# First-chunk keys without copies, bounds buffers cleared on VectorE, and some gelu casts on ScalarE, in a fused attention and MLP kernel

## The chip, the cores and the metric

The kernel runs on one core of a Trainium2 chip. The metric is the device time of one execution in microseconds, median over runs. The engines are TensorE (PE, with its weight loads as PEld), VectorE (DVE), ScalarE (ACT), GpSimd (POOL) and SyncE (SP); transfers are issued from SP's and ScalarE's queues.

## What is computed

Attention over 4 batches, 8 heads, 768 positions and 64 elements a head, in which a query sees the first `n_global` keys and a window of `n_local` keys behind it, with a slope by distance for each head; then a two-layer MLP with exact gelu over the 3072 rows of 512.

```python
scores = scale * np.matmul(q, k.transpose(0, 1, 3, 2))
keep = is_global | is_local                     # key < n_global, or 0 <= q - k < n_local
scores = np.where(keep, scores + bias, -1e9)    # bias = -slope_h * distance
a = softmax(scores);  x = np.matmul(a, v)       # then (B*S, H*D) = (3072, 512)
h = x @ w_in                                    # 512 -> 2048
g = 0.5 * h * (1.0 + erf(h / sqrt(2)))
out = g @ w_out                                 # 2048 -> 512
```

The weights come as 64-bit words; the kernel decodes them itself.

## The kernel before

The rows are cut into 12 chunks `c` of 256 queries, three to a batch. The attention of a chunk goes by four pairs of heads `p`. `scores_pair` multiplies queries and keys in two halves `j` of 128 queries, for each head `hh` and each half `a` of 64 queries. The keys of such a half are 192 columns: 64 near, 32 global and 96 near. In the chunks that begin a batch they are picked out of a row of keys with copies behind it (`kr`, with `KW + 96` columns). One reduction on VectorE (L373) adds the masks `pens` and takes the row maxima into `nmax`. `exps` takes exponentials on ScalarE (L402) with sums `su`; then come the sum's inverse (L404, L405) and the scaling of `n` (L411), on VectorE in chunks 0 and 1 and on GpSimd after that. `flip` transposes on TensorE (L423) and copies to `pt` on ScalarE (L427), `av_pair` multiplies with the values (L461) and splits the result into a high and a low part of `x` in fp16 (L503 or L510 on ScalarE, L191 on VectorE).

The MLP goes by slices `s` of 256 of the 2048 columns, eight of them, in steps `T`: first the slices of chunks 0 and 1 in turn, then the other chunks. `m1` is the first layer (L537, and L531 for chunks 0 and 1 from slice 2 on), `gelu` takes the gelu on ScalarE into `gr` (L553) and splits it into `gh` (L554) and `gl` (L192) on VectorE, `m2` is the second layer (L581, L566). Each slice's weights come in four pieces; `split_weights` and `part_weights` decode a piece with one instruction on ScalarE (L227), three on VectorE (L233, L235, L237), a cast on ScalarE (L247) and a rest on VectorE (L192), into `winh`, `winl`, `wouth`, `woutl`. Slice 0 is decoded beside the attention of chunks 0 and 1, the others up to about step 14. `warm` issues products whose result nobody reads, as many as the table `FILL` says, between those of the first attention.

`consts` builds the masks: row and column numbers by GpSimd, casts on VectorE (L150, L151), the two limits by a transfer (L80, used from L86 on), and eight scaled masks `pens` (L168). The buffers `xtop`, `xlow`, `wtop` and `wlow` hold running bounds from step 15 on; they are cleared in `consts` by GpSimd.

Each engine serves its own list in order. The lists are not the order of the code: a scheduler lays the instructions out by its own estimate of their times, with some orders given by hand (`after`, `behind`, `table`). A small change of the code can so change the lists elsewhere.

## Time and profile before

| | us |
|---|---|
| median of 3 runs | 648.76 (648.11 to 650.12) |
| the profiled execution, its own time | 647.65 |
| its span, first to last instruction | 645.8 |
| TensorE busy | 628.7 (97%) |
| VectorE busy | 369.2 (57%) |
| ScalarE busy | 313.0 (48%) |
| GpSimd busy | 80.4 (12%) |

Times in the trace are counted from the span's start. A busy share is a mean over stages: VectorE is busy without a break from about 50 to 120 us and half idle after that. The chain of work that ended last says which engine was waited for.

### The profile page before, as it was taken

The numbers are of one execution on the slowest core, as the hardware profiler recorded it, in microseconds if no ns is written. First come the engines' busy times: TensorE is split into PE (matmuls) and PEld (weight loads), VectorE is DVE, ScalarE is ACT, GpSimd is POOL, SyncE is SP. The second block draws the span as 40 slices with busy tenths as digits, with TensorE's granted clock in tenths as the row PEclk, the third lists the DMA queues.
The fourth block names the chain that finished last, engine by engine and source line by source line (L and its number), as shares of the span: only waits on it lengthen the run. The fifth ranks groups of instructions, "written<-read, shape, count | busy, mean of one in ns | idle before, by whom it ended". The sixth has DMA issues, their size and how long they took to land.

```text
span 645.8 us, 14522 instructions
## 1 busy us (share of the span) xinstructions
PE 628.7 (97%) x5712; PEld 424.3 (66%) x5712; DVE 369.2 (57%) x1160; ACT 313.0 (48%) x757; POOL 80.4 (12%) x175
## 2 busy tenths in 40 slices
PE   8998999999999999999999999999999999999995
PEld 5555544457777676676776767677776767767663
DVE  8989999955546546436436436435435445342622
ACT  3786586735535526526526436355355355362210
POOL 3000005301202102101002022021011021020000
PEclk9998999999999999999999999999999999999998
DMA  8949825314504415304235145034064062000001
GB/s 256 261 177 266 262 73 192 115 37 144 171 24 143 119 56 162 113 37 147 80 94 165 49 124 165 11 138 133 17 172 128 37 172 66 33 2 1 34 1 38
DMA packets 66187, 71.27 MB, mean 110 GB/s; under 512 B 32704, under 2 KB 49344, under 8 KB 66112
## 3 DMA queue, kind: packets, MB, share of 16 engines
q1 hardware_dynamic: 61664, 62.93, 32.2%
q10 hardware_dynamic: 4448, 7.34, 3.2%
q8 instruction: 47, 0.77, 0.5%
q14 instruction: 28, 0.23, 0.1%
HBM read 63.97 MB, written 6.29 MB: 109 GB/s over the span
## 4 chain that ended last, share of the span: by engine, by line
PE 84%; DVE 9%; ACT 4%; issue 1%; DMA 1%; POOL 0%; POOLq 0%; ACTq 0%; DVEq 0%
PE h L537 33%; PE acc L581 32%; PE av L461 5%; PE t L423 5%; PE s L362 4%; PE h L531 2%; PE acc L566 2%; DVE wb L235 2%; ACT n L402 1%; DVE wb L237 1%; DVE wb L233 1%; DVE n L373 1%; DVE gl L192 1%; DVE ta L150 1%; DVE winl L192 1%
## 5 line engine op out<-in xcount | busy, mean ns | idle before, releaser
L537 PE MATMUL h<-x,winh 128*128 128x256 f16 x1344 | 228.3, 274 | 0.9 <-ACT x L503 0.4
L537 PE MATMUL h<-x,winl 128*128 128x256 f16 x672 | 184.0, 274 | 0.0
L554 DVE TENSOR_SCALAR gh<-gr 128x512 f16<-128x512 f32 x96 | 42.7, 445 | 213.6 <-ACT gr L553 213.6
L537 PEld LDWEIGHTS <-winh 128*128 128x128 f16 x1344 | 131.5, 98 | 32.9 <-issue 1.4
L411 POOL TENSOR_SCALAR n<-n,su 128x192 f32<-128x192 f32 (+1 forms) x160 | 75.2, 489 | 494.3 <-ACT n L402 240.2
L553 ACT ACTIVATE gr<-h 128x512 f32<-128x512 f32 x96 | 57.3, 597 | 153.9 <-issue 87.3
L581 PE MATMUL acc<-wouth,gl 128*128 128x512 f16 x336 | 127.0, 379 | 1.0 <-DVE gl L192 1.0
L581 PE MATMUL acc<-wouth,gh 128*128 128x512 f16 x336 | 127.5, 380 | 0.1
L581 PE MATMUL acc<-woutl,gh 128*128 128x512 f16 x336 | 127.3, 379 | 0.0
L581 PEld LDWEIGHTS <-gh 128*128 128x128 f16 x672 | 64.2, 98 | 66.0 <-issue 4.3
L427 ACT COPY pt<-t 128x384 f32<-128x384 f32 x96 | 45.1, 475 | 93.7 <-PE t L423 92.0
L537 PEld LDWEIGHTS <-winl 128*128 128x128 f16 x672 | 66.1, 98 | 9.7 <-issue 0.8
L192 DVE SCALAR_TENSOR_TENSOR gl<-gr,gh 128x512 f16<-128x512 f32 x96 | 66.7, 694 | 8.5
L402 ACT ACTIVATE n<-n,mn 128x192 f32<-128x192 f32 (+1 forms) x144 | 62.1, 432 | 4.1 <-DVE mn L373 3.9
L581 PEld LDWEIGHTS <-gl 128*128 128x128 f16 x336 | 32.9, 98 | 41.0 <-DVE gl L192 1.5
L373 DVE CUSTOM_DVE_ANT_0 n<-s,pens 128x192 f32<-128x192 f32 (+1 forms) x192 | 54.9, 341 | 0.1
L423 PE MATMUL t<-ident,n 128*128 128x128 f32 x288 | 47.8, 276 | 3.2 <-DVE n L411 2.4
L461 PE MATMUL av<-pt,vr 64*64 64x64 f32 (+2 forms) x1312 | 42.4, 250 | 2.0 <-ACT pt L427 2.0
L461 PEld LDWEIGHTS av<-pt,vr 64*64 64x64 f32 (+1 forms) x1312 | 35.4, 134 | 11.5 <-issue 8.0
L423 PEld LDWEIGHTS t<-ident,n 128*128 128x128 f32 x288 | 34.7, 142 | 8.5 <-DVE n L411 2.4
L362 PE MATMUL s<-kr,qr 64*64 64x192 f32 (+2 forms) x752 | 39.1, 323 | 0.7 <-DMA kr<-kT 0.7
L261 DVE SCALAR_TENSOR_TENSOR wand<-c,wand 128x128 int32<-128x128 int32 x128 | 37.5, 293 | 2.7
(108 smaller groups left out, 595.9 us busy)
## 6 DMA issues: line engine op xcount, KB each, us to landing
w<-w SPq DMA_DIRECT2D x32, 512.0 KB, 6.3
c<-w SPq DMA_DIRECT2D x32, 512.0 KB, 5.6
out<-o ACTq DMA_DIRECT2D x23, 256.0 KB, 2.0
qr<-qT SPq DMA_DIRECT2D x11, 512.0 KB, 4.2
vr<-v SPq DMA_DIRECT2D x22, 256.0 KB, 4.4
kr<-kT SPq DMA_DIRECT2D x16, 320.0 KB, 4.9
vr<-v SPq DMA_DIRECT2D x19, 192.0 KB, 2.9
kr<-kT SPq DMA_DIRECT2D x36, 64.0 KB, 3.3
```

Of the source, the lines that this page charges most:

```text
L192: return self.nc.vector.scalar_tensor_tensor(out=out, in0=in_, scalar=scale, in1=hi, op0=ALU.mult, op1=ALU.subtract)
L362: ins = nc.tensor.matmul(out, lhsT=lhs, rhs=rhs, start=True, stop=True).ins
L373: ins = nc.vector.tensor_tensor_reduce(out=nn[:, j * NK:j * NK + n], in0=sp[hh][:, j, 0:n], in1=self.pens[:, 2 * p + hh, o:o + n], scale=- ...
L402: self.table(nc.scalar.activation(out=nn, in_=nn, func=AF.Exp, bias=mn[:, i:i + 1], scale=-1.0, accum_out=su[:, i:i + 1]))
L411: ins = eng.tensor_scalar(out=nn, in0=nn, scalar1=su[:, i:i + 1], scalar2=0.0, op0=ALU.mult, op1=ALU.add)
L423: self.last_t = nc.tensor.transpose(tp[:, i, :], nn[:, o:o + P], self.ident).ins
L427: ins = nc.scalar.copy(pt, tp).ins
L461: ins = nc.tensor.matmul(out, lhsT=lhs, rhs=rhs, start=start, stop=stop, skip_group_check=True).ins
L537: ins = nc.tensor.matmul(hp[:, f, :], lhsT=w[:, d, fs], rhs=x[:, d, e, :], start=n == 0, stop=n == 3 * NP - 1).ins
L553: self.table(nc.scalar.activation(out=gr, in_=hp, func=AF.Gelu, scale=1.0 / (WS * XS)))
L554: nc.vector.tensor_scalar(out=gh, in0=gr, scalar1=GS, scalar2=None, op0=ALU.mult)
L581: ins = nc.tensor.matmul(acc, lhsT=g[:, f, ks], rhs=w[:, f, :], start=s == 0 and n == 0, stop=(s == NST - 1 or (c, s) == (NCH - 1, NST - 2 ...
```

## The change

Three edits, and the order of instructions that follows from them.

Chunk 0 keeps only its 256 columns of keys, without copies behind them, so two transfers (96 and 32 columns of all four pairs) are not issued. In its second half (`c == 0`, `j == 1`) each product of 192 columns becomes three, of 64, 32 and 96 columns, with the same weights and neighbouring results. `FILL` loses its entry between the two halves of pair 0, and gives 5 and 7 products instead of 4 and 9 behind pairs 0 and 1. The four bounds buffers are cleared on VectorE at step 14 instead of on GpSimd in front. And from slice 2 on the cast to `gh` is done by ScalarE for chunks 0 and 1, which is twelve steps.

```diff
-FILL = {(0, 0, 0): 4, (0, 0, 1): 4, (0, 1, 1): 9, (0, 2, 1): 4, (0, 3, 1): 4, (1, 0, 1): 4}
+FILL = {(0, 0, 1): 5, (0, 1, 1): 7, (0, 2, 1): 4, (0, 3, 1): 4, (1, 0, 1): 4}
...
-        for m in (self.xtop, self.xlow, self.wtop, self.wlow):
-            nc.gpsimd.memset(m, 0.0)
...
-        kr = self.es.tile([P, NP, KW + 96], F32, name="kr0")
+        kr = self.es.tile([P, NP, CT], F32, name="kr0")
...
-        nc.sync.dma_start(kr[:, 0, 0:CT], dap(self.kT, 0, [[S, P], [1, CT]]))
+        nc.sync.dma_start(kr[:, 0], dap(self.kT, 0, [[S, P], [1, CT]]))
         nc.scalar.dma_start(qr[:, 1:NP], dap(self.qT, P * S, [[S, P], [P * S, NP - 1], [1, CT]]))
-        nc.sync.dma_start(kr[:, :, CT:CT + 96], dap(self.kT, 0, every + [[1, 96]]))
-        nc.sync.dma_start(kr[:, :, CT + 96:], dap(self.kT, 0, every + [[1, NG]]))
-        nc.sync.dma_start(kr[:, 1:NP, 0:CT], dap(self.kT, P * S, [[S, P], [P * S, NP - 1], [1, CT]]))
+        nc.sync.dma_start(kr[:, 1:NP], dap(self.kT, P * S, [[S, P], [P * S, NP - 1], [1, CT]]))
...
+                    elif c == 0:
+                        x = 2 * P - HQ if a else NG
+                        parts = [(out[:, 0:NX], kt[hr, x:x + NX]), (out[:, NX:NX + NG], kt[hr, 0:NG]),
+                                 (out[:, NX + NG:], kt[hr, NC:2 * NC])]
...
+                    for out, rhs in parts:
+                        ins = nc.tensor.matmul(out, lhsT=lhs, rhs=rhs, start=True, stop=True).ins
...
-        nc.vector.tensor_scalar(out=gh, in0=gr, scalar1=GS, scalar2=None, op0=ALU.mult)
+        if STEPS[t][0] < CAT and STEPS[t][1] > 1:
+            nc.scalar.activation(out=gh, in_=gr, func=AF.Copy, scale=GS)
+        else:
+            nc.vector.tensor_scalar(out=gh, in0=gr, scalar1=GS, scalar2=None, op0=ALU.mult)
...
+            if T == 14:
+                for m in (self.xtop, self.xlow, self.wtop, self.wlow):
+                    self.behind(self.nc.vector.memset(m, 0.0))
```

The lists change in many places. First VectorE's, at the first two pairs of heads (`n_0` to `n_3` are the scores of heads 0 to 3 of chunk 0, `su` their sums). Before:

```order
L404 TENSOR_SCALAR su_0_262<-su_0_262 128x4
L373 ISA n_2_313,nmax<-s_2_296,pens 128x128
...
L405 RECIPROCAL su_0_262<-su_0_262 128x4
L373 ISA n_3_316,nmax<-s_3_297,pens 128x192
...
L411 TENSOR_SCALAR n_0_279<-n_0_279,su_0_262 128x128
```

Now:

```order
L404 TENSOR_SCALAR su_0_256<-su_0_256 128x4
L405 RECIPROCAL su_0_256<-su_0_256 128x4
L411 TENSOR_SCALAR n_0_278<-n_0_278,su_0_256 128x128
...
L373 ISA n_2_318,nmax<-s_2_295,pens 128x128
```

The scaling of heads 0 and 1 has moved ahead of the reductions of heads 2 and 3.

Then VectorE's, where the second chunk begins (`n_0`, `n_1` and `su_0` are now those of chunk 1, `n_7` is chunk 0's last head, `wb_1` to `wb_3` are pieces of the first slice). Before, the reductions of chunk 1's heads 0 and 1 stand ahead of all this:

```order
L411 TENSOR_SCALAR n_7_435<-n_7_435,su_3_419 128x192
L192 SCALAR_TENSOR_TENSOR winl_330<-wb_1_393,winh_329 128x512
L233 TENSOR_SCALAR wb_2_451<-w_2_186 128x512
L404 TENSOR_SCALAR su_0_477<-su_0_477 128x4
L191 TENSOR_TENSOR x<-av_2_466,x 128x256
L235 SCALAR_TENSOR_TENSOR wb_2_451<-w_2_186,wb_2_451 128x512
L405 RECIPROCAL su_0_477<-su_0_477 128x4
L237 ISA wb_2_451<-w_2_186,wb_2_451 128x1024
L411 TENSOR_SCALAR n_0_492<-n_0_492,su_0_477 128x192 x2
```

Now:

```order
L411 TENSOR_SCALAR n_7_456<-n_7_456,su_3_432 128x192
L190 SCALAR_TENSOR_TENSOR winl_335<-wb_1_406,winh_334 128x512
L231 TENSOR_SCALAR wb_2_472<-w_2_180 128x512
L233 SCALAR_TENSOR_TENSOR wb_2_472<-w_2_180,wb_2_472 128x512
L235 ISA wb_2_472<-w_2_180,wb_2_472 128x1024
L373 ISA n_0_513,nmax<-s_0_499,pens 128x192
...
L404 TENSOR_SCALAR su_0_498<-su_0_498 128x4
L405 RECIPROCAL su_0_498<-su_0_498 128x4
L411 TENSOR_SCALAR n_0_513<-n_0_513,su_0_498 128x192 x2
```

The four reductions of chunk 1's first pair now stand behind the decoding of piece 2, directly ahead of the sum that waits for their exponentials. (Lines behind the diff's first edits are numbered a few lower or higher in the new kernel.)

Last, ScalarE's list at a step with exponentials between the gelu and its cast (`n_0`, `n_1` are scores of chunk 2). Before:

```order
L553 ACTIVATE gr_1187<-h_1172 128x512
L402 ACT_TABLE_LOAD
L402 ACTIVATE n_0_1140,su_0_1129<-n_0_1140,nmax 128x192 x2
L402 ACTIVATE n_1_1143,su_0_1129<-n_1_1143,nmax 128x192 x2
L247 ACTIVATE wouth_993<-wb_3_1057 128x512
L247 ACTIVATE winh_1096<-wb_0_1101 128x512
```

Now:

```order
L553 ACTIVATE gr_1208<-h_1193 128x512
L402 ACT_TABLE_LOAD
L402 ACTIVATE n_0_1161,su_0_1150<-n_0_1161,nmax 128x192 x2
L402 ACTIVATE n_1_1164,su_0_1150<-n_1_1164,nmax 128x192 x2
L245 ACTIVATE winh_1117<-wb_0_1122 128x512
L225 ACTIVATE w_2_238<-w_2_238 128x512
L225 ACTIVATE w_3_240<-w_3_240 128x512
L555 ACTIVATE gh_1206<-gr_1208 128x512
```

The cast to `gh` stands behind the exponentials and three weight instructions.

## Rows read from the trace of the kernel before

**Rows 1.** The page's chain of work that ended last, by engine

```profile
PE 84%; DVE 9%; ACT 4%; issue 1%; DMA 1%; POOL 0%; POOLq 0%; ACTq 0%; DVEq 0%
```

**Rows 2.** Timeline of VectorE, 0 to 16 us: start, us, engine, line, operation

```profile
1.77 4.04 DVE L150 CAST ta<-tb 128x320 f32<-128x320 int32 x1 [0.22 <-POOL tb L147]
...
6.19 0.16 DVE L86 CAST nn_f<-nn_w 128x4 f32<-128x4 int32 x1
...
10.48 0.29 DVE L373 CUSTOM_DVE_ANT_0 n<-s,pens 128x128 f32<-128x128 f32 x1
```

**Rows 3.** Timeline of GpSimd: the last of the four clears

```profile
4.67 0.96 POOL L170 MEMSET wlow<- 128x1024 f16 x1
```

**Rows 4.** Timeline of ScalarE's queue, and transfers to 40 us with median time to landing

```profile
0.74 0.42 ACTq L80 DMA_DIRECT2D nn_w<-limits  x1
...
nn_w<-limits ACTq DMA_DIRECT2D x1, 2.0 KB, 3.7
```

**Rows 5.** The chain in order of time, 0 to 67 us: start, us, what

```profile
10.81 1.76 ACT n L402 x8
...
14.81 0.56 ACT w L227
15.36 0.37 ACT pt L427
...
16.21 0.91 PE s L362 x12
...
18.67 0.96 PE av L461 x14
...
28.89 0.38 DVE x L191
...
29.96 0.64 DVE wb L237
...
31.52 0.34 DVE wb L233
...
32.45 0.60 DVE wb L235
```

**Rows 6.** Timeline of VectorE: the scaling of four pairs ends where these begin

```profile
20.18 0.17 DVE L404 TENSOR_SCALAR su<-su 128x4 f32<-128x4 f32 x1 [1.32 <-ACT n L402]
...
21.45 0.69 DVE L192 SCALAR_TENSOR_TENSOR winl<-wb,winh 128x512 f16<-128x512 f32 x1
...
31.43 0.42 DVE L233 TENSOR_SCALAR wb<-w 128x512 int32<-128x512 int32 x1
...
36.60 0.42 DVE L233 TENSOR_SCALAR wb<-w 128x512 int32<-128x512 int32 x1
```

**Rows 7.** Timeline of TensorE, 66 to 140 us: its gaps, with who ended them

```profile
100.95 0.44 PE L423 MATMUL t<-ident,n 128*128 128x128 f32 x2 [0.76 <-POOL n L411]
...
122.28 0.59 PE L531 MATMUL h<-x,winh 128*128 128x512 f16 x2 [0.42 <-DVE x L191]
```

**Rows 8.** Groups by line: the page's, and those of 5 to 60 us by shape

```profile
L554 DVE TENSOR_SCALAR gh<-gr 128x512 f16<-128x512 f32 x96 | 42.7, 445 | 213.6 <-ACT gr L553 213.6
...
L247 ACT ACTIVATE winh<-wb 128x512 f16<-128x512 f32 x5 | 3.1, 624 | 0.1
```

**Rows 9.** TensorE's timeline at 29.78, and busy time by window with PEclk, granted clock

```profile
29.78 0.43 PE L461 MATMUL av<-pt,vr 128*64 128x128 f32 x2 [1.42 <-ACT pt L427]
...
31.00:32.00 1.00, 1.00 (x11) 0.43 (x4) 1.00 (x5) 0.26 (x1) 0.00 (x0) 0.50 0.93 340
```

**Rows 10.** TensorE's timeline: six transposes; and their weight loads, 5 to 60 us

```profile
14.19 1.00 PE L423 MATMUL t<-ident,n 128*128 128x128 f32 x6 [0.26 <-DVE n L411]
...
L423 PEld LDWEIGHTS t<-ident,n 128*128 128x128 f32 x48 | 5.7, 144 | 5.0 <-DVE n L411 2.4 <-ACT pt L427 0.7 <-issue 0.7
```

**Rows 11.** The chain in order of time, 67 to 160 us

```profile
111.18 2.71 PE h L531 x12
...
114.59 1.28 ACT L402
```

More of the change, by code (lines that the diff above doesn't have):

```diff
@@ L267, in load_first @@
         nc = self.nc
-        kr = self.es.tile([P, NP, KW + 96], F32, name="kr0")
+        kr = self.es.tile([P, NP, CT], F32, name="kr0")
         qr = self.es.tile([P, NP, CT], F32, name="qr0")
         vr = self.es.tile([P, 4, DM], F32, name="vr0")
-        every = [[S, P], [P * S, NP]]
         nc.sync.dma_start(qr[:, 0], dap(self.qT, 0, [[S, P], [1, CT]]))
-        nc.sync.dma_start(kr[:, 0, 0:CT], dap(self.kT, 0, [[S, P], [1, CT]]))
+        nc.sync.dma_start(kr[:, 0], dap(self.kT, 0, [[S, P], [1, CT]]))
         nc.scalar.dma_start(qr[:, 1:NP], dap(self.qT, P * S, [[S, P], [P * S, NP - 1], [1, CT]]))
-        nc.sync.dma_start(kr[:, :, CT:CT + 96], dap(self.kT, 0, every + [[1, 96]]))
-        nc.sync.dma_start(kr[:, :, CT + 96:], dap(self.kT, 0, every + [[1, NG]]))
-        nc.sync.dma_start(kr[:, 1:NP, 0:CT], dap(self.kT, P * S, [[S, P], [P * S, NP - 1], [1, CT]]))
+        nc.sync.dma_start(kr[:, 1:NP], dap(self.kT, P * S, [[S, P], [P * S, NP - 1], [1, CT]]))
         self.vr[0] = vr
@@ L351, in scores_pair @@
                     if c == 0 and j == 0:
-                        out, lhs, rhs = sp[hh][:, 0, 0:P], qq[hr, 0:P], kt[hr, 0:P]
-                    elif first and j == 0:
-                        out, rhs = out[:, 0:P], kt[hr, 0:P]
-                    else:
-                        if first:
-                            rhs = pairs(kt[hr, :], 192 if a else 288, -96 if a else -192, NC)
-                        elif j == 0:
-                            rhs = pairs(kt[hr, :], 96, 96 if a else -96, NC)
-                        else:
-                            rhs = pairs(kt[hr, :], KW + 192 * a, -96 if a else 96, NC)
-                    ins = nc.tensor.matmul(out, lhsT=lhs, rhs=rhs, start=True, stop=True).ins
-                    if prev is not None:
-                        self.after(ins, prev, "heads and halves in turn")
-                    prev = ins
+                        parts = [(sp[hh][:, 0, 0:P], kt[hr, 0:P])]
+                        lhs = qq[hr, 0:P]
+                    elif c == 0:
+                        x = 2 * P - HQ if a else NG
+                        parts = [(out[:, 0:NX], kt[hr, x:x + NX]), (out[:, NX:NX + NG], kt[hr, 0:NG]),
+                                 (out[:, NX + NG:], kt[hr, NC:2 * NC])]
+                    elif first and j == 0:
+                        parts = [(out[:, 0:P], kt[hr, 0:P])]
+                    elif first:
+                        parts = [(out, pairs(kt[hr, :], 192 if a else 288, -96 if a else -192, NC))]
+                    elif j == 0:
+                        parts = [(out, pairs(kt[hr, :], 96, 96 if a else -96, NC))]
+                    else:
+                        parts = [(out, pairs(kt[hr, :], KW + 192 * a, -96 if a else 96, NC))]
+                    for out, rhs in parts:
+                        ins = nc.tensor.matmul(out, lhsT=lhs, rhs=rhs, start=True, stop=True).ins
+                        if prev is not None:
+                            self.after(ins, prev, "heads and halves in turn")
+                        prev = ins
             if (c, p, j) in FILL:
```

## The prediction

> **What bounds the kernel now.** I read the chain of work that ended last first: 84% of the span is TensorE [rows 1]. From about 62 us on its products follow one another almost without a gap; later work that is made shorter on another engine is worth only the gaps it closes. Then I read the chain's first 67 us and the timelines of the first 60: there TensorE waits for a ring in which VectorE reduces the scores of a pair of heads (L373), ScalarE takes the exponentials (L402), VectorE scales them (L404 to L411), TensorE transposes and multiplies, and VectorE decodes weight words (L233, L235, L237) in between. So the time is the length of the head, plus TensorE's gaps behind it, plus fixed TensorE work. The change touches the first two.
>
> **No clearing on GpSimd.** VectorE's cast of the row numbers (L150) takes 4.04 us for 320 columns [rows 2], while GpSimd clears four buffers, the last until 5.63 [rows 3]. Without them the cast should fall well under 1 us. Not all of that is gained: the third instruction behind it, L86, needs the two limits, whose transfer is issued at 0.74 and lands 3.7 us later, at 4.44 [rows 4]; no edit moves it. From L86 at 6.19 to the first reduction at 10.48 VectorE does 4.29 us of masks [rows 2], so the first reduction comes at 4.44 + 4.29 = 8.73: **1.75 us earlier**. What GpSimd still does in front (an iota, the identity) can stretch the cast by a microsecond or so and costs nothing, as the limits come later. The four clears return on VectorE at step 14, beside TensorE's gapless run and behind the last decoding; I cost them at nothing.
>
> **Keys kept once.** Two transfers of 262 KB together go, and the transfer of the other pairs' keys moves up on SP's queue; the first products already lie ahead of the masks, so this is only cover. For the price: in each of four pairs, the four products of 192 columns become twelve of 64, 32 and 96, three in a row on the same half of the array. The trace has no such row. The nearest are a whole old block, two wide and four such products in 0.91 us, and seven smaller products (14 entries) in 0.96 [rows 5]. The low bound for the twelve is then about 0.5 us, as now; at the second row's 0.069 us per entry, 24 entries are 1.65. I take 1.30, between them and nearer to that row. For the first two pairs it lies beside other work. For the third and fourth the new TensorE order puts nine and eight of the twelve ahead of the value products that ScalarE now waits for.
>
> **The order that comes with it.** This is the largest term. The new VectorE list takes the scaling of pair 0 ahead of the reductions of pair 1, and decodes piece 2 of the first slice ahead of the second chunk's first reductions. VectorE then stands idle through each pair's exponentials, where it used to have something queued between. I lay the new lists out with the old durations. Four exponentials take 1.76 us [rows 5] and begin 0.33 behind the first reduction (10.81 against 10.48); sum, reciprocal and four scalings take 21.45 - 20.18 = 1.27 [rows 6]; with a handshake of 0.03 or so.
> Pair 0: reductions 8.73, exponentials 9.06 to 10.82, scaled at 12.12. Pair 1: its reductions only then, exponentials 12.45 to 14.21, scaled at 15.51. ScalarE decodes a piece (0.56) and copies the transposes (0.37), to 15.14. Pair 2: TensorE needs 0.40 for the first value product, 0.42 for the wide score products, 0.98 for nine pieces and 0.96 for the other value products: 17.90. ScalarE's cast of x now stands ahead of the exponentials: 18.2 to 19.95; scaled at 21.25. Before, that was 21.45 [rows 6], so only 0.2 of the 1.75 are left. Pair 3: ScalarE's two weight instructions and a copy (1.48) to 21.43, TensorE 0.40 + 0.42 + 0.87 + 0.96 to 24.1, cast and exponentials to 26.1, scaled at 27.4.
> Second chunk: VectorE first does 0.60 + 0.34 + 0.60 + 0.64 = 2.18 of decoding, to 29.6; then reductions, exponentials to 31.7, scaled at 33.0. Before, the scaling ended and L233 began at 31.43 [rows 6]: **1.6 us later**. Its next pair: decoding and x, 0.60 + 0.34 + 0.38 + 0.60 + 0.64 = 2.56, to 35.56; with 0.33 + 1.76 + 1.30 scaled at 38.95 against 36.60 [rows 6]: **2.35 us later**. From there on both lists run alike up to the dense stretch, which I let begin 2.4 us later. With the twelve products at 0.5 instead of 1.30 the two TensorE passages save 0.8 x 17/12 = 1.1, and it is +1.3.
> [...]
>
> **Casts on ScalarE.** Twelve casts leave VectorE, at 0.445 each [rows 8], 5.3 us in the stretch in which it is busy without a break. ScalarE pays some 0.62 for each, as for a cast of the same size to winh [rows 8], 7.4 us in all, from its idle time. VectorE's lead closes two gaps of TensorE, 0.76 waiting for scaled probabilities and 0.42 for x [rows 7]: **-1.18 us**. The gaps near 60 us come ahead of the first moved cast and stay. Where exponentials stand between gelu and cast, the cast ends 1.28 + 1.76 + 0.62 + 2 x 0.56 + 0.62 = 5.4 us behind gelu. What hides it is the new TensorE order: twelve products of the step before and 24 of the first layer, 3 x 2.71 = 8.1 us [rows 11]. If that cover is gone, VectorE waits for the cast too, with its decoding queued behind gl.
>
> **Sum.** +2.4 - 1.18 = +1.2 us. The profiled execution (647.65, span 645.8) is 1.1 below the median of the three runs; I add the difference to the median: 648.76 + 1.2 = **650.0** (648.9 and a span of 647.0 by the profile).
>
> **Rivals.** *The lead carries through.* The idle stretches that I laid out are filled by something I did not see, and the head keeps its 1.75: 648.76 - 1.75 - 1.18 = 645.8. For it: the old chain begins with the cast and goes almost without waits to the masks. Against it: VectorE's list is served in order, and the waits stand in it by name.
> [...]
> *The moved cast is late.* At the two steps with exponentials between, TensorE waits for gh and gl, 0.62 + 0.60 each: 650.0 + 2.4 = 652.4. Against it is the cover of 2.7 us.
> [...]
>
> **How the numbers follow.** Forecast 0.50, lead carried 0.17, clock 0.22, late cast 0.06, loads 0.05. A measurement of this kernel can tell about 0.3%, 1.95 us, from no change: 646.8 to 650.7 counts as the same. Of the forecast's 0.50 I put 0.41 inside, 0.08 above, 0.01 below. Faster 0.17 + 0.01 = 0.18; same 0.41; slower 0.08 + 0.22 + 0.06 + 0.05 = 0.41. The range goes from 646.0, in the middle of the lead carried, to 653.5, which leaves out a second fall of the clock and the worst of the loads, some 0.17 together. The forecast alone would be 648.9 to 651.5.
>
> **What would show it.** In the profile of the changed kernel L150 should be under 1 us, with VectorE waiting at L86 until about 4.4, and the first reduction near 8.7. VectorE should stand idle for about 1.1 us behind the reductions of both first pairs. The second chunk's first scaling should end near 33.0 and its second near 39.0. TensorE's gaps of 0.76 and 0.42 near 100 and 122 us should be gone. The twelve products should take 0.5 to 1.65. I am wrong if the gelu of the first step starts earlier than now (the layout is wrong), if the clock falls between 15 and 27 us, or if TensorE waits for gh or gl between 70 and 130 us.

## The result, and the profile after

The changed kernel takes 655.75 us (median of 6 runs), the kernel before 648.38 (6 runs beside it): a ratio of 1.0107, interval 1.0089 to 1.0125. It is **slower, by 7.4 us** between the medians, and the forecast of 650.0, its range (646.0 to 653.5) included, was too low. The profiled execution is 656.0 with a span of 654.2, which is 8.4 more than the span of before.

First the page: the share of TensorE in the chain that ended last, beside [rows 1], and the busy times.

```profile
PE 630.9 (96%) x5771; PEld 426.9 (65%) x5771; DVE 364.7 (56%) x1152; ACT 319.6 (49%) x769; POOL 71.0 (11%) x171
PE 82%; DVE 8%; ACT 6%; issue 2%; DMA 1%; DVEq 0%; ACTq 0%; SPq 0%
```

TensorE's busy time rose by only 2.2 us, so most of the 8.4 is TensorE waiting. Where, the starts of the same gelu tell, step by step: the first begins at 43.02 instead of 39.80 (+3.22), the one at the entry of the dense stretch (TensorE's run from there on, in which its products follow one another almost without a gap) at 70.67 instead of 66.89 (+3.78), one at 105.56 instead of 102.17 (+3.39), and the one behind the last decoding at 157.68 instead of 149.34 (**+8.34**). From there on the two kernels run alike. So there are two losses, one in the head and one between 105 and 150 us, and each was followed by itself.

**The head.** VectorE's timeline, 0 to 42 us (start, us, engine, line, operation, and what ended the idle time ahead), answers [rows 2] and [rows 6]:

```profile
1.78 0.47 DVE L150 CAST ta<-tb 128x320 f32<-128x320 int32 x1 [0.21 <-POOL tb L147]
...
4.39 0.17 DVE L86 CAST nn_f<-nn_w 128x4 f32<-128x4 int32 x1 [1.63 <-DMA nn_w<-limits]
...
8.63 0.28 DVE L373 CUSTOM_DVE_ANT_0 n<-s,pens 128x128 f32<-128x128 f32 x1
...
10.75 0.17 DVE L404 TENSOR_SCALAR su<-su 128x4 f32<-128x4 f32 x1 [1.06 <-ACT n L402]
...
21.13 0.68 DVE L190 SCALAR_TENSOR_TENSOR winl<-wb,winh 128x512 f16<-128x512 f32 x1
...
27.44 0.68 DVE L190 SCALAR_TENSOR_TENSOR winl<-wb,winh 128x512 f16<-128x512 f32 x1
...
29.95 0.35 DVE L373 CUSTOM_DVE_ANT_0 n<-s,pens 128x192 f32<-128x192 f32 x1
...
33.58 0.69 DVE L190 SCALAR_TENSOR_TENSOR woutl<-wb,wouth 128x512 f16<-128x512 f32 x1
...
36.18 0.35 DVE L373 CUSTOM_DVE_ANT_0 n<-s,pens 128x192 f32<-128x192 f32 x1
...
39.80 0.68 DVE L190 SCALAR_TENSOR_TENSOR woutl<-wb,wouth 128x512 f16<-128x512 f32 x1
```

The cast is short, VectorE waits for the limits, and the first reduction comes at 8.63 instead of 10.48. The L190 rows stand right behind the scaling of pairs 2 and 3 and of chunk 1's first two pairs. The lead of 1.85 is down to 0.32 at 21.13 (21.45 before) and a loss of 2.15 at 33.58 (31.43 before) and 3.2 at 39.80 (36.60 before). TensorE's timeline shows the same from the other side; these are its gaps, one ahead of each pair's value products. Before, they were 0.58, none, none and 1.42, the last in [rows 9]:

```profile
15.06 0.43 PE L461 MATMUL av<-pt,vr 128*64 128x128 f32 x2 [2.46 <-ACT pt L427]
...
21.31 0.43 PE L461 MATMUL av<-pt,vr 128*64 128x128 f32 x2 [1.59 <-ACT pt L427]
...
27.61 0.43 PE L461 MATMUL av<-pt,vr 128*64 128x128 f32 x2 [1.66 <-ACT pt L427]
...
33.69 0.43 PE L461 MATMUL av<-pt,vr 128*64 128x128 f32 x2 [1.85 <-DVE n L411]
```

They begin 6.2 us apart: that is the length of the ring for one pair in the new order.

**The step at 122 us.** ScalarE's timeline from 118 to 127 us:

```profile
121.40 0.72 ACT L225 ACTIVATE w<-w 128x512 int32<-128x512 uint32 x1 [2.54 <-DMA w<-w]
121.99 0.58 ACT L553 ACTIVATE gr<-h 128x512 f32<-128x512 f32 x1
122.59 1.28 ACT L402 ACT_TABLE_LOAD   x1
...
125.66 0.61 ACT L555 ACTIVATE gh<-gr 128x512 f16<-128x512 f32 x1
```

and TensorE's at the same place:

```profile
120.81 1.50 PE L461 MATMUL av<-pt,vr 128*64 128x128 f32 x44
122.13 1.38 PE L362 MATMUL s<-kr,qr 64*64 64x192 f32 x16
126.33 0.39 PE L569 MATMUL acc<-wouth,gh 128*128 128x512 f16 x1 [2.82 <-ACT gh L555]
...
128.49 0.63 PE L569 MATMUL acc<-woutl,gh 128*128 128x512 f16 x1
...
130.61 0.60 PE L531 MATMUL h<-x,winh 128*128 128x512 f16 x2
```

The gelu did not start when its last product was there (117.43) but at 121.99. Ahead of it in ScalarE's list stands a weight instruction (L225, the fourth piece of slice 7) that waited 2.54 us for its transfer. Behind the gelu come the table load and four exponentials, and only then the cast. TensorE had about 5.1 us of other work and then stood. From the start of the score block at 122.13 to the next product it took 4.20, where the same block took 0.76 in the kernel before,

```profile
118.20 0.83 PE L362 MATMUL s<-kr,qr 64*64 64x192 f32 x16
118.96 0.39 PE L566 MATMUL acc<-wouth,gh 128*128 128x512 f16 x1
```

so **3.44 are lost**. Behind the gap the products follow at 0.43 instead of 0.216, and the busy time by window has the granted clock (the third number from a row's end) at 0.50:

```profile
128.00:129.00 1.00, 1.00 (x4) 0.38 (x3) 1.00 (x7) 0.21 (x1) 1.00 (x4) 0.50 1.13 283
```

Eight products at that rate cost **1.65** more. The transfer was late because its issue was: on SP's queue it waited for VectorE, by the waits of SP between 100 and 123 us (us in total, times, longest):

```profile
SPq L200 <- DVE wb L235: 17.7, 3, 10.2
```

VectorE had to read the staging buffer of an earlier piece before it could be filled again. The transfer went out at 117.68, just behind that, and landed 3.7 us later.

**The balance** of the 4.56 us between the entry and 150 us: 3.44 + 1.65 for the late cast and the clock behind it; 0.92 for two score blocks of chunk 2 that the new order takes in two parts (82.40 and 86.42, 92.51 and 93.52), each 0.46 longer than in one; -1.18 for the two gaps of [rows 7], which are gone as forecast; and -0.27 that is not put down to anything.

### The profile page after: what moved, and what is told of

Same layout as the page of the kernel before. It is cut to its first block, busy times and chain, and to the rows that moved or that the text cites. A ratio compares the mean times of both kernels' runs of the same rounds, so it can differ in the third digit from the quotient of the medians.

```text
span 654.2 us, 14626 instructions
## 1 busy us (share of the span) xinstructions
PE 630.9 (96%) x5771; PEld 426.9 (65%) x5771; DVE 364.7 (56%) x1152; ACT 319.6 (49%) x769; POOL 71.0 (11%) x171
## 4 chain that ended last, share of the span: by engine, by line
PE 82%; DVE 8%; ACT 6%; issue 2%; DMA 1%; DVEq 0%; ACTq 0%; SPq 0%
PE h L537 33%; PE acc L584 32%; PE av L461 5%; PE t L423 4%; PE s L362 4%; ACT n L402 2%; PE acc L569 2%; DVE wb L233 2%; PE h L531 2%; DVE wb L235 1%; DVE wb L231 1%; ACT w L225 1%; DVE gl L190 1%; DVE n L411 1%; ACT L402 1%
## 5 line engine op out<-in xcount | busy, mean ns | idle before, releaser
L557 DVE TENSOR_SCALAR gh<-gr 128x512 f16<-128x512 f32 x84 | 37.3, 444 | 204.4 <-ACT gr L553 204.3
L411 POOL TENSOR_SCALAR n<-n,su 128x192 f32<-128x192 f32 (+1 forms) x160 | 69.4, 453 | 512.7 <-DVE su L405 223.7
L190 DVE SCALAR_TENSOR_TENSOR gl<-gr,gh 128x512 f16<-128x512 f32 x96 | 66.7, 694 | 21.0 <-ACT gh L555 12.1
L373 DVE CUSTOM_DVE_ANT_0 n<-s,pens 128x192 f32<-128x192 f32 (+1 forms) x192 | 54.8, 341 | 0.4 <-PE s L362 0.3
L362 PE MATMUL s<-kr,qr 64*64 64x192 f32 (+5 forms) x816 | 42.6, 309 | 0.0
```

Of the source, the lines that this page charges most:

```text
L190: return self.nc.vector.scalar_tensor_tensor(out=out, in0=in_, scalar=scale, in1=hi, op0=ALU.mult, op1=ALU.subtract)
L362: ins = nc.tensor.matmul(out, lhsT=lhs, rhs=rhs, start=True, stop=True).ins
L373: ins = nc.vector.tensor_tensor_reduce(out=nn[:, j * NK:j * NK + n], in0=sp[hh][:, j, 0:n], in1=self.pens[:, 2 * p + hh, o:o + n], scale=- ...
L411: ins = eng.tensor_scalar(out=nn, in0=nn, scalar1=su[:, i:i + 1], scalar2=0.0, op0=ALU.mult, op1=ALU.add)
```

## The experiments

Offsets are those of the profiled execution against the kernel before: the gelu that there starts at 66.89 (entry of the dense stretch) and the one at 149.34 (behind the last decoding). Ratios come from several runs of both kernels and carry the verdicts; they need not be the quotient of two medians to the last digit, and a single profiled execution lies up to 2 us off its median.

| run | median us | ratio to before, interval | entry | behind decoding |
|---|---|---|---|---|
| the change | 655.75 | 1.0107 [1.0089, 1.0125] | +3.78 | +8.34 |
| only_clear | 646.89 | 0.9977 [0.9965, 0.9989] | -1.21 | -1.18 |
| only_keys | 655.08 | 1.0108 [1.0086, 1.0129] | +5.37 | +5.69 |
| only_cast | 653.34 | 1.0065 [1.0044, 1.0086] | +2.87 | +7.07 |
| no_cast | 653.07 | 1.0055 [1.0034, 1.0076] | +4.90 | +5.57 |
| after_stg4 | 652.68 | 1.0065 [1.0049, 1.0082] | +4.93 | +5.36 |
| after_ghnow | 652.28 | 1.0071 [1.0058, 1.0084] | +3.33 | +4.17 |
| keys_oldorder | 649.63 | 1.0017 [1.0004, 1.0031] | +0.48 | +1.45 |
| keys_oldorder2 | 649.32 | 1.0013 [1.0002, 1.0024] | +1.68 | +1.83 |
| clear_order | 647.18 | 0.9984 [0.9971, 0.9998] | -1.01 | -0.95 |
| no_cast_fill0 | 651.94 | 1.0058 [1.0044, 1.0071] | +2.75 | +4.09 |
| pieces_in_old_order | 648.83 | 1.0007 [0.9993, 1.0022] | -0.38 | -0.08 |
| old_products_in_new_order | 650.48 | 1.0039 [1.0025, 1.0053] | +3.32 | +3.41 |
| clear_cast_best | 646.25 | 0.9963 [0.995, 0.9976] | -0.84 | -1.08 |
| repaired | 647.27 | 0.9985 [0.9974, 0.9995] | +0.11 | -1.08 |
| all_in_old_order | 647.91 | 0.999 [0.9977, 1.0003] | +0.59 | +0.34 |

### One edit at a time

**only_clear**: the kernel before with nothing but the clears moved.

```diff
-        for m in (self.xtop, self.xlow, self.wtop, self.wlow):
-            nc.gpsimd.memset(m, 0.0)
...
+            if T == 14:
+                for m in (self.xtop, self.xlow, self.wtop, self.wlow):
+                    self.behind(self.nc.vector.memset(m, 0.0))
```

> Only the clearing is moved; keys and casts are as before, and so is VectorE's list up to the last scaling of chunk 2. Theory (the keys edit made the lists of the head, and they ate the lead): with the old lists the first reduction comes about 1.8 us earlier, near 8.7, and the whole head keeps it, so the gelu of the first step starts near 38.0 instead of 39.80 and the time is 648.4 - 1.8 = 646.6. Rival (something else paces the head, a transfer or a ring): the first reduction is early, the gelu of the first step is not, 648.4.

It is 1.5 us faster. The rows are those of the change: L150 takes 0.48, L86 waits for the limits until 4.11, and the lead of about 1.5 at the first gelu (38.27) is still 1.2 at the end of the decoding. By itself, in the old order, the lead is carried. It is smaller than in the change, whose first reduction comes at 8.63: here that reduction, at 8.95, waited 0.52 us for its scores, and TensorE ahead of them 0.94 for a transfer of keys.

**only_keys**: the kernel before with only the keys' edit: the two transfers left out, the products in pieces, the new `FILL`.

```diff
-        kr = self.es.tile([P, NP, KW + 96], F32, name="kr0")
+        kr = self.es.tile([P, NP, CT], F32, name="kr0")
...
+                    elif c == 0:
+                        x = 2 * P - HQ if a else NG
+                        parts = [(out[:, 0:NX], kt[hr, x:x + NX]), (out[:, NX:NX + NG], kt[hr, 0:NG]),
+                                 (out[:, NX + NG:], kt[hr, NC:2 * NC])]
```

> Only the keys edit with its fillers; GpSimd clears in front and VectorE casts, as before. The head's list on VectorE is then that of the kernel after. Theory: the head loses what the kernel after lost at the entry of the dense stretch (3.8) and the lead of 1.85 that the kernel after had besides, so the first acc product behind gl comes near 61.65 + 5.6 = 67.3, and the time is 654.0; no wait for gh. Rival (the pieces cost only what they take on TensorE, 4 x 0.7, half of it covered): 649.8.

7.0 us slower by the ratio, nearly all of it ahead of the dense stretch (+5.37 of +5.69 in the profiled execution, the fastest of four). The scheduler gives the new order of VectorE to this edit alone, so the order belongs to the keys, not to the clearing. It costs more here than it does in no_cast (below), by more than the 1.5 of the lead that is missing; its profiled execution has the granted clock at 0.50 from 18 to 24 us, where the change's has it at 1.00.

**only_cast**: the kernel before with only the casts moved.

```diff
-        nc.vector.tensor_scalar(out=gh, in0=gr, scalar1=GS, scalar2=None, op0=ALU.mult)
+        if STEPS[t][0] < CAT and STEPS[t][1] > 1:
+            nc.scalar.activation(out=gh, in_=gr, func=AF.Copy, scale=GS)
+        else:
+            nc.vector.tensor_scalar(out=gh, in0=gr, scalar1=GS, scalar2=None, op0=ALU.mult)
```

> Only the casts move to ScalarE; the head is that of before. ScalarE's list in the dense stretch is that of the kernel after: the weight words w7_2 and w7_3 stand ahead of the gelu of step 14. Theory (the list and the late transfer of w7_3 make the cast late, whatever the head does): one wait of TensorE for gh of about 3 us near 122 us with a fall of the granted clock behind it, 5.1 us in all, less the two gaps of 1.18 and with 0.65 for score products that are split in two: 648.4 + 4.6 = 653.0. Rival (it was late only because the longer head had moved the transfers): no wait for gh, 647.2.

4.2 us slower by the ratio, with both gaps of [rows 7] gone. The same late step is there, first ScalarE's timeline (116 to 126 us, two rows):

```profile
120.16 0.71 ACT L227 ACTIVATE w<-w 128x512 int32<-128x512 uint32 x1 [2.21 <-DMA w<-w]
120.77 0.59 ACT L553 ACTIVATE gr<-h 128x512 f32<-128x512 f32 x1
```

then TensorE's, one gap of the head and the one at the step:

```profile
14.18 1.00 PE L423 MATMUL t<-ident,n 128*128 128x128 f32 x6 [1.00 <-DVE n L411]
...
125.10 0.61 PE L569 MATMUL acc<-wouth,gh 128*128 128x512 f16 x1 [2.82 <-ACT gh L555]
```

The first product there already takes 0.61 where the change has 0.39, and the granted clock is 0.50 from 126 to 128 us. The edit loses 4.2 us in the dense stretch of the profiled execution (7.07 - 2.87). The entry's 2.87 is a surprise, since up to 66 us its lists are those of before; it is taken up in the last section.

**no_cast**: the change without the moved casts.

```diff
-        if STEPS[t][0] < CAT and STEPS[t][1] > 1:
-            nc.scalar.activation(out=gh, in_=gr, func=AF.Copy, scale=GS)
-        else:
-            nc.vector.tensor_scalar(out=gh, in0=gr, scalar1=GS, scalar2=None, op0=ALU.mult)
+        nc.vector.tensor_scalar(out=gh, in0=gr, scalar1=GS, scalar2=None, op0=ALU.mult)
```

> The kernel after with the casts back on VectorE; keys and clearing as after, and so is the list of the head. By the two traces the casts cost the kernel after 4.6 us net from 61 us on (a wait for gh with the slow clock behind it 5.1, score products split in two 0.9, less 1.2 for two gaps closed and 0.3). Theory (head and casts are two separate costs): 655.75 - 4.6 = 651.2, with no wait for gh and the gaps of 0.76 and 0.42 back. Rival (the shorter lists of VectorE had paid for part of the head): 652.5 or more.

By the ratios (1.0107 against 1.0055) the casts cost 3.4 us and 3.6 stay. The dense stretch loses 0.67 instead of 4.56; the gap of 0.76 is back, and that of 0.42 for `x` is 1.05. The split is less sharp than the theory had it: the median, 653.07, lies in the rival's range, and the interval of what stays (2.2 to 4.9 us) takes in the forecast's 2.4. That the head costs more than that is clear only with no_cast_fill0 below (2.9 to 4.6).

### The late cast

**after_stg4**: the change with four staging buffers for weight words instead of three.

```diff
-        self.stg = pool("stg", 3)
+        self.stg = pool("stg", 4)
```

> The kernel after with four instead of three staging buffers for the weight words; ScalarE's list is the same word for word. Theory (the transfer of w7_3 waits for a staging buffer that VectorE frees at 117.6, and the gelu of step 14 stands behind it): w7_3 lands several us earlier, ScalarE does not wait ahead of that gelu, TensorE's gap of 2.82 and the fall of the clock behind it go, 655.75 - 5.1 = 650.7. Rival (the exponentials between gelu and cast are enough to make it late): the gap stays, at 2 us or more, 655.7.

ScalarE's list is the same word for word. Its timeline from 115 to 128 us now reads

```profile
119.30 1.23 ACT L225 ACTIVATE w<-w 128x512 int32<-128x512 uint32 x2
120.42 0.57 ACT L553 ACTIVATE gr<-h 128x512 f32<-128x512 f32 x1
...
124.08 0.61 ACT L555 ACTIVATE gh<-gr 128x512 f16<-128x512 f32 x1
```

and TensorE's

```profile
124.75 0.39 PE L569 MATMUL acc<-wouth,gh 128*128 128x512 f16 x1 [0.66 <-ACT gh L555]
```

Both weight instructions run without a wait, the gap falls from 2.82 to 0.66, and the products behind it follow at 0.216 again, with the granted clock at 1.00 from 126 to 131 us. The dense stretch loses 0.43 instead of 4.56 in the profile, and the median falls by 3.1. So the wait for the transfer was the cause of most of the loss, with the clock behind it. What is left of the gap, 0.66, is a wait for the cast, ahead of which the exponentials still stand. The time misses the theory's 650.7 by 2 us; the head of this execution accounts for 1.15 of that (+4.93 at the entry instead of +3.78).

**after_ghnow**: the change with the cast ahead of the table load and the exponentials (`self.table` orders an activation with the gelu).

```diff
-            nc.scalar.activation(out=gh, in_=gr, func=AF.Copy, scale=GS)
+            self.table(nc.scalar.activation(out=gh, in_=gr, func=AF.Copy, scale=GS))
```

> The kernel after with each moved cast ahead of the next exponentials by a manual order; three staging buffers as in after, so the transfer of w7_3 still comes late and the gelu of step 14 still waits for it. Theory (transfer and exponentials are late only together): ScalarE still waits some 2.5 us ahead of that gelu, but the cast ends 3.2 us earlier, TensorE waits under 0.5 us for gh, the clock stays up: 651.2. Rival (the transfer alone is enough): a gap of 2 us or more, 655.

The transfer is as late as in the change, but the cast now follows the gelu at once (ScalarE, 112 to 124 us):

```profile
120.16 0.72 ACT L225 ACTIVATE w<-w 128x512 int32<-128x512 uint32 x1 [2.44 <-DMA w<-w]
120.77 0.57 ACT L553 ACTIVATE gr<-h 128x512 f32<-128x512 f32 x1
121.37 0.63 ACT L555 ACTIVATE gh<-gr 128x512 f16<-128x512 f32 x1
122.02 1.28 ACT L402 ACT_TABLE_LOAD   x1
```

TensorE no longer waits for `gh`; between 66 and 140 us its only wait is the one for `x`, which [rows 7] has with 0.42 and which has grown:

```profile
PE h L531 <- DVE x L189: 1.3, 1, 1.3
```

The median falls to 652.28, where the theory had 651.2; the dense stretch loses 0.84 instead of 4.56. The two runs together say that it took both, the late transfer *and* the exponentials, to make the cast so late: with either taken away most of the loss goes.

### The head

**keys_oldorder**: no_cast with VectorE's two places put back, so that the scaling of pair 0 stands behind the reductions of pair 1 and that of pair 3 behind chunk 1's first ones, with piece 2 decoded later.

```diff
+DEFER = ((0, 0), (0, 3))
...
+        if self.tail is not None:
+            tail, self.tail = self.tail, None
+            self.scale(*tail, self.last_dve)
...
+        if (c, p) in DEFER:
+            self.tail = c, every, su, mn
+            return
+        self.scale(c, every, su, mn)
...
-                    self.split_weights(s, i)
+                    if (s, i) != (0, 2):
+                        self.split_weights(s, i)
...
+            if T == DECODE[0, 2]:
+                self.split_weights(0, 2)
```

> As no_cast, with two places of VectorE's list of the head put back by hand: the reductions of pair 1 ahead of the scaling of pair 0, and the reductions of chunk 1's first pair ahead of the scaling of pair 3 and of the decoding of piece 2. Key products in pieces, fillers and TensorE's order stay. Theory (VectorE's order eats the lead, 2.2 to 3 us): about 648.5. Rival (TensorE's order behind the pieces, nine and eight of them ahead of the value products, with fewer fillers and the clock, is what costs): the same as no_cast, 651.

649.63: 3.4 us of no_cast's loss are gone by the medians, 2.5 by the ratios, and the entry is +0.48 instead of +4.90. The order of two places on VectorE carries most of the head's loss, as the prediction had it; 0.17% remains. The two entries overstate it, as the granted clock from 6 us to the entry is 0.94 in this execution and 0.87 in that of no_cast.

**keys_oldorder2**: the same, with the value products of the first two pairs behind the scores of the next but one, and the cast of `x` behind the exponentials, as before.

```diff
+        if c == 0 and p < 2:
+            self.after(ins, self.last_s, "behind the scores of the next but one pair")
...
+            if c == 0 and p < 2:
+                self.after(xc.ins, self.last_table, "behind the exponentials")
...
-            self.att(T, "av")
+            if T >= START[0] + 4:
+                self.att(T, "av")
...
+            if T < START[0] + 4:
+                self.att(T, "av")
```

> As keys_oldorder, and by hand also TensorE's and ScalarE's order of the first attention as before the change: all score pieces of pairs 2 and 3 ahead of the value products of pairs 0 and 1, and the casts of their x behind the exponentials. Pieces and fillers stay. Theory (the orders cost, the pieces themselves little): each pair's ring falls from 6.2 us to about 5.2, and the time is 647.4, 0.5 above only_clear. Rival (the pieces' own time and the fewer fillers cost): 649.6, as keys_oldorder.

649.32, no further gain. The rival's time came. Putting back these places on TensorE and ScalarE did not bring the rest, which lies elsewhere (the square below puts it down to the pieces).

**clear_order**: only_clear with VectorE's two places as in the change.

```diff
+                if p == 0 and c == 1:
+                    self.after(ins.ins, self.last_dec, "behind piece 2")
+                if p == 1 and c == 0 and hh == 0 and j == 0:
+                    self.after(ins.ins, self.last_dve, "behind the scaling of pair 0")
```

> The converse: as only_clear (old keys, four products of 192 columns, old fillers), but by hand the reductions of pair 1 behind the scaling of pair 0, and those of chunk 1's first pair behind the decoding of piece 2, as in the kernel after. Theory (VectorE's order costs): 646.9 + 2.5 = 649.4, the scaling of chunk 1's second pair some 2 us later than in only_clear. Rival (pieces and TensorE's order cost): 646.9.

Only 0.3 us slower than only_clear, as the rival had it. This run did not isolate the order: the scheduler answered by moving fifteen first-layer products ahead of transposes on TensorE. Chunk 1's first two scalings ended 3.0 and 4.3 us later, but the first gelu came only 1.6 later. So VectorE's places cost little where TensorE's list adapts like this; what they cost with TensorE's list held, it leaves open.

**no_cast_fill0**: no_cast with `FILL` as before.

```diff
-FILL = {(0, 0, 1): 5, (0, 1, 1): 7, (0, 2, 1): 4, (0, 3, 1): 4, (1, 0, 1): 4}
+FILL = {(0, 0, 0): 4, (0, 0, 1): 4, (0, 1, 1): 9, (0, 2, 1): 4, (0, 3, 1): 4, (1, 0, 1): 4}
```

> As no_cast, with the old fillers: four between the halves of pair 0, four behind it and nine behind pair 1, instead of none, five and seven. The lists are else the same but for two reductions of pair 1 that move ahead of the scaling of pair 0. Theory (the fillers are not the cause): 652 to 653, as no_cast. Rival (with fewer fillers the granted clock falls at 15 to 23 us, and that is what the head loses): the clock stays up there, the first gelu 2 us earlier, 650.5.

651.94 (1.0058), as no_cast (1.0055). The new numbers of `FILL` are not what makes the order, and by the ratios not what costs. The rival's signs did come in the profiled execution: the granted clock is 1.00 from 15 to 27 us, where no_cast has 0.72, and the first gelu comes 1.65 earlier. The ratios, from five and seven executions, do not show that gain; a small one they leave open.

The next two pin the lists of TensorE, VectorE and ScalarE up to about 65 us by a table of instruction numbers, so that products and order are changed one without the other (old `FILL`, no moved casts, clears moved, in both):

```diff
+PIN = (...)
...
+        for row in PIN:
+            for a, b in zip(row, row[1:]):
+                self.after(ins[f"I-{b}"], ins[f"I-{a}"], "as in the list")
```

**pieces_in_old_order**: products in pieces, lists of only_clear.

> The keys edit and the moved clearing with the old fillers, and with the lists of TensorE, VectorE and ScalarE up to about 65 us pinned, instruction for instruction, to those of only_clear; three pieces stand where one product stood, and two transfers of keys are missing. Theory (the lists cost, the pieces do not): the head of only_clear plus two blocks on the path, 2 x 0.56 us at most, 647 to 648. Rival (the pieces' own time on TensorE costs, the lists matter little): 651 or more, as no_cast_fill0.

**old_products_in_new_order**: products of 192 columns, lists of no_cast_fill0.

> The converse: only_clear, with four products of 192 columns for each pair, its lists up to about 65 us pinned, instruction for instruction, to those of no_cast_fill0. Theory (the lists cost): 651, near the 651.9 of no_cast_fill0, with the scaling of chunk 1's second pair near 39 us. Rival (the pieces cost): 647.2, near only_clear.

With only_clear and no_cast_fill0 they make a square (times 648 us, against the kernel before):

| | old order | new order |
|---|---|---|
| old products | -1.5 | +2.5 |
| pieces | +0.5 | +3.8 |

The order costs 3.3 to 4.0 us, the pieces 1.3 to 2.0, and the two nearly add. The intervals are about 0.8 us to either side of each entry, so the order's cost is clear and that of the pieces barely. "Pieces" stands here for the whole edit of the keys, with the two transfers left out. pieces_in_old_order came between its theory (647 to 648) and its rival (651), the other where its theory had it. The order costs that with the clock alike: from 15 to 27 us the granted clock is 1.00 in all four profiled executions, and from 6 us to the entry it is 0.94 and 0.95 with the old products, 0.97 and 0.97 with the pieces. Between these entries lie 4.53 and 3.13 us. TensorE's timeline of pieces_in_old_order, from the first pair's value products to the fourth's:

```profile
14.29 0.43 PE L507 MATMUL av<-pt,vr 128*64 128x128 f32 x2 [0.24 <-ACT pt L473]
14.65 1.54 PE L408 MATMUL s<-kr,qr 64*128 64x128 f32 x28
...
29.44 0.43 PE L507 MATMUL av<-pt,vr 128*64 128x128 f32 x2 [1.42 <-ACT pt L473]
```

and that of only_clear:

```profile
14.24 0.43 PE L459 MATMUL av<-pt,vr 128*64 128x128 f32 x2 [0.38 <-ACT pt L425]
14.61 0.98 PE L360 MATMUL s<-kr,qr 64*128 64x128 f32 x12
...
28.26 0.65 PE L459 MATMUL av<-pt,vr 128*64 128x128 f32 x2 [1.42 <-ACT pt L425]
```

A pair's scores take 28 entries in 1.54 us instead of 12 in 0.98, that is 0.56 more. TensorE has no gap in between in either kernel until the last, so two pairs make the passage 15.15 instead of 14.02. That is the price of the pieces, paid in full where TensorE is the bound of the ring; it explains 1.1 of the 2.0 in the old order, and the rest is inside the intervals. In the new order with the old products TensorE has a gap ahead of each pair, as in the change:

```profile
15.47 0.43 PE L503 MATMUL av<-pt,vr 128*64 128x128 f32 x2 [1.03 <-ACT pt L469]
...
21.32 0.43 PE L503 MATMUL av<-pt,vr 128*64 128x128 f32 x2 [1.66 <-ACT pt L469]
...
27.20 0.43 PE L503 MATMUL av<-pt,vr 128*64 128x128 f32 x2 [1.70 <-DMA vr<-v]
...
33.26 0.43 PE L503 MATMUL av<-pt,vr 128*64 128x128 f32 x2 [1.83 <-DVE n L453]
```

(The releaser named in the third row is a transfer of the values; the same gap has ScalarE's `pt` in the change.)

### What is best

**clear_cast_best**: the clears moved, the casts on ScalarE ahead of the exponentials, four staging buffers, and the keys as before.

```diff
-        self.stg = pool("stg", 3)
+        self.stg = pool("stg", 4)
...
-        nc.vector.tensor_scalar(out=gh, in0=gr, scalar1=GS, scalar2=None, op0=ALU.mult)
+        if STEPS[t][0] < CAT and STEPS[t][1] > 1:
+            self.table(nc.scalar.activation(out=gh, in_=gr, func=AF.Copy, scale=GS))
+        else:
+            nc.vector.tensor_scalar(out=gh, in0=gr, scalar1=GS, scalar2=None, op0=ALU.mult)
```

> Old keys; clearing on VectorE at step 14; casts on ScalarE, each by a manual order ahead of the next exponentials; four staging buffers. Theory (the cast costs only by the late transfer and the exponentials between): no wait for gh, the gaps of 0.76 and 0.42 closed, 646.9 - 1.2 = 645.7, faster than both kernels. Rival (casts on ScalarE hold up exponentials or weights instead, and TensorE waits for those): 647 or more.

646.25, 0.37% faster than the kernel before and the fastest of all. The lead over only_clear (0.9977) is inside the intervals, so nearly all of it is the clearing; the moved casts, without their wait, are no more than a small gain. The theory had both gaps closed; the one of 0.76 is, and the one for `x` stays at 0.40.

**repaired**: keys_oldorder2 with the same casts and buffers.

```diff
-        self.stg = pool("stg", 3)
+        self.stg = pool("stg", 4)
...
+            self.table(nc.scalar.activation(out=gh, in_=gr, func=AF.Copy, scale=GS))
```

> All three edits of the change with everything put right that the theory blames: the lists of the head as in keys_oldorder2, each cast ahead of the next exponentials, four staging buffers. Theory: keys_oldorder2 less 0.7 (the two gaps of 1.18 closed, 0.5 back for split score products), 646.7 if keys_oldorder2 is 647.4; not faster than clear_cast_best with its old keys. Rival (the pieces free the transfers of the head and are worth something once the lists are right): under 645.5.

**all_in_old_order**: all edits, with the old `FILL`, these casts and buffers, and the lists of the head pinned to those of clear_cast_best.

```diff
+PIN = (...)
...
+                self.after(ins[f"I-{b}"], ins[f"I-{a}"], "as in the list")
```

> All three edits, old fillers, the lists of the head pinned to those of clear_cast_best, each moved cast ahead of the next exponentials, four staging buffers: clear_cast_best with pieces in place of its four products and without the two transfers of copied keys. Theory (pieces are nearly free once the lists are right, the transfers were hidden anyway): 646.3 to 647.3 against the 646.25 of clear_cast_best. Rival (the pieces themselves cost some 2.5 us in the head, as keys_oldorder2 left open): 648.5 or more.

647.27 and 647.91. With its order and its casts repaired the change comes out even with the kernel before, or 0.15% faster; all_in_old_order, between its theory and its rival, is 1.7 us slower than clear_cast_best with the same lists of the head, which is the price of the pieces once more. The keys' edit found no gain in any form that ran. In none of them were the transfers left out without the pieces, so what they alone are worth was not measured. The start of the head shows that it is something: with the clears moved and the old keys the first reduction waits for its scores and comes at 8.95, 9.53 and 9.43 (only_clear, old_products_in_new_order, clear_cast_best), and without the transfers at 8.59, 8.65 and 9.05 (pieces_in_old_order, no_cast_fill0, all_in_old_order).

## Why the prediction was wrong, point by point

**No clearing: right.** L150 fell to 0.47, VectorE waits at L86 until 4.39, the first reduction comes at 8.63 (forecast 8.73). only_clear carries 1.5 us of it to the end. The rival that the lead carries through holds for this edit alone.

**Pieces: right in kind, a little too dear.** A score block with pieces takes 0.56 longer than one without (forecast: 1.30 for the twelve instead of 0.5, so 0.8 more). The weight loads run beside the products, as one row of TensorE's loads in the changed kernel, 5 to 60 us by shape (busy us, mean ns of one), shows:

```profile
L362 PEld LDWEIGHTS s<-kr,qr 64*64 64x64 f32 x160 | 6.3, 133 | 1.0 <-issue 0.5
```

Twenty-four such loads one after another would be 3.2, and the whole block of 28 entries takes 1.54 in pieces_in_old_order. The chance of 0.05 for the loads was for 24 of them, 0.14 each as in [rows 10], with none beside a product: by my estimate a block of 3.4 and a time of 653.0. No run shows such a block, so this rival is dead. The two transfers were more than the "cover" for which I took them: once the masks are early, the first reduction comes 0.36, 0.88 and 0.38 earlier without them, in three pairs of runs with the same lists (pieces_in_old_order and only_clear, no_cast_fill0 and old_products_in_new_order, all_in_old_order and clear_cast_best).

**The order: right in kind, mis-sized.** The layout held closely for the first chunk: pair 2 scaled at 21.13 (forecast 21.25), pair 3 at 27.44 (27.4). Chunk 1's pairs came at 33.58 and 39.80 instead of 33.0 and 38.95. Their reductions (L373) began at 29.95 and 36.18 where I had 29.6 and 35.56: the decoding ahead of them took 2.51 and 2.60 instead of 2.18 and 2.56. From there to the end of the scaling it took 3.63 and 3.62 instead of 3.39, as I had priced chunk 1 with rows of chunk 0, where half of the score tiles have 128 columns and not 192. That makes 0.85 of the miss by 39.80. At the entry it was **+3.78 where the sum had +2.4**. The other 0.5 comes between 40 and 71 us, where TensorE has the lower clock for longer: over 52 to 59 us, in the changed kernel and then in the kernel before, the busy time by window has a granted clock of 0.51 and 0.84.

```profile
52.00:59.00 7.00, 6.02 (x34) 4.20 (x34) 6.17 (x16) 5.09 (x10) 0.00 (x0) 0.51 0.86 255
52.00:59.00 7.00, 6.61 (x79) 5.10 (x78) 5.80 (x12) 5.50 (x13) 0.00 (x0) 0.84 1.11 285
```

What the clock alone cost there was not separated from what the order moved there. The square gives the head's terms by ratios: order and pieces together 5.3 (4.0 and 1.3, or 3.3 and 2.0), less the 1.5 of the clearing, which is +3.8.

**The clock in the first attention.** The chance of 0.22 for the clock was for a fall to 0.50, as [rows 9] show it behind a gap. By my layout TensorE stands about 1.2 us ahead of the second pair's value products, at 21.43, and at 0.50 the 2.65 us behind that would take 2.65 more: by my estimate 652.6 instead of 650.0. In the profiled execution of the change the granted clock is 1.00 from 15 to 27 us, though the gaps (2.46, 1.59, 1.66) were longer than 1.2. In the four other profiled executions with these lists of the head it fell: over 15 to 27 us it is 0.72 in no_cast, after_stg4 and only_keys, and 0.86 in after_ghnow. So this rival did not make the time of the profiled execution, and the order costs without it, as the square shows; but it came in four of five executions of these lists, and in neither of the two with the new order and the old `FILL` (no_cast_fill0, old_products_in_new_order). What it adds to the medians was not separated. See the last section.

**Split score blocks: not foreseen.** Two blocks of chunk 2 are taken in two parts, 0.92 us; in no_cast both are whole (86.95 and 93.05). I had followed TensorE's list in the head and at the two gaps, not in between.

**Casts: the gain was right, the cover was the failed step.** Both gaps are gone, -1.18 as forecast. But "What hides it is the new TensorE order: twelve products of the step before and 24 of the first layer" was read from another step with exponentials, where it held (gelu at 93.40, the cast done at 99.30, wanted at 101.67). It did not hold at step 14, the step at 122 us. There TensorE had, by its timeline, twelve second-layer products, the value products and a score block, about 5.1 us and not 8.1. And I counted 5.4 us from the gelu, taking it to start with its last product. It started 4.56 us behind that, since in the new list a weight instruction stands ahead of it whose transfer waits for a staging buffer. In the order I had quoted that the weight instructions moved ahead of the cast, but did not follow which of them moved ahead of the *gelu*, nor to the wait that the last of them had in the kernel before, harmless behind the exponentials (ScalarE, 113 to 124 us):

```profile
120.83 0.68 ACT L227 ACTIVATE w<-w 128x512 int32<-128x512 uint32 x1 [1.45 <-DMA w<-w]
```

The late cast was a rival of mine, at a chance of 0.06 and +2.4 us; it came, at one step instead of two, and cost 5.1, of which 1.65 is the clock behind its gap, which I had not put into its price.

**The sum.** In the profiled executions the forecast was +1.2 and the result +8.34: 1.38 of the difference is the head, 5.09 the late cast with its clock, 0.92 the split blocks, -0.27 not put down. Without the late cast, after_stg4 (652.68) and after_ghnow (652.28) lie inside the range and 2 to 3 us above the forecast, by the head. Against the medians the miss is 5.75, as I had added 1.1 for a profiled execution below its median, and that of the change lies 0.25 above its own.

## What to carry to other kernels

Before work is moved to an engine with slack, write out the list of that engine from the last input of the moved step to its output, with every wait that stands in between, and read the cover at *that* step from the other engine's timeline, not from a like one. An instruction that waits for a transfer was harmless behind the critical step here and dear ahead of it; when a scheduler is free to swap them, pin the one that matters or give the transfer another buffer. And an edit that splits a few instructions can cost more by the order that it brings than by itself: here 3.3 to 4.0 us against 1.3 to 2.0, so time the order and the instructions apart.

## What the runs showed of the hardware that was not expected

The granted clock falls at different places in different executions of the same lists. no_cast has the list of the change for the head; the windows at 16 us are, for the change and then for no_cast,

```profile
16.00:17.00 1.00, 1.00 (x23) 0.88 (x23) 0.86 (x2) 0.00 (x0) 0.00 (x0) 1.00 1.11 347
```

```profile
16.00:17.00 1.00, 1.00 (x17) 0.78 (x16) 0.86 (x2) 0.00 (x0) 0.00 (x0) 0.50 1.11 343
```

In the change TensorE had stood for 2.46 us ahead of it, and the granted clock stays at 1.00; in no_cast it had stood for 1.65, and the clock is 0.50 until about 22.7. The entry of the dense stretch then is +4.90 instead of +3.78. only_cast, whose lists up to 66 us are those of before, shows the same:

```profile
16.00:17.00 1.00, 1.00 (x6) 0.53 (x5) 0.97 (x3) 0.09 (x1) 0.00 (x0) 0.50 1.09 348
```

behind a gap of 1.00, where the kernel before had a gap of 0.26 at that place and a granted clock of 1.00. The entry came 2.87 later in that execution. The length of a gap alone does not tell here whether the clock falls: it is 1.00 behind a gap of 2.46 and 0.50 behind gaps of 1.65 and 1.00. Why it falls in one execution and not in the next stays open. So an us or two of this head are a matter of the single execution, and one profile cannot price its order: that took the ratios of the square.
